# Chunked attention with two MoE layers on one core: the first eight blocks' value rows loaded by query group, their memory rows copied on GpSimd, and a planner that counts eight transfers in flight

## The chip, the cores and the metric

One core of a Trainium2 chip runs the whole kernel. The metric is the device time of one execution in microseconds (us), the median of several runs. The profile that is read here is one execution of the kernel before, recorded by the hardware profiler. The engines are named as in the profile: PE (TensorE matmul), PEld (TensorE weight load), DVE (VectorE), ACT (ScalarE), POOL (GpSimd) and SP (SyncE, which issues the transfers; SPq is its queue).

## The reference

Attention works on chunks of 32 queries. Each chunk sees 8 memory rows, 16 rows to its left, its own 32 rows and 8 rows to its right (64 rows in all); then two layers with a hidden width of 2048 follow, in float32.

```python
batch, n_heads, seq, head_dim = (4, 8, 768, 64); n_mem = 8
chunk, left_ctx, right_ctx = (32, 16, 8)
k_full = np.concatenate([mem_k, k_ctx], axis=2)
v_full = np.concatenate([mem_v, v_ctx], axis=2)
scores = scale * np.matmul(q_c, k_full.transpose(0, 1, 3, 2))
a = np.exp(scores - np.max(scores, axis=-1, keepdims=True))
a = a / (np.sum(a, axis=-1, keepdims=True) + 1e-09)
out[:, :, c_start:c_end] = np.matmul(a, v_full)
...
h = x @ w_in                               # 3072 x 512 by 512 x 2048
y = (h * np.clip(h + 3.0, 0.0, 6.0) / 6.0) @ w_out
# second layer: the same shapes, with a squared gate in place of the clipped one
```

## The kernel before, in words

**Attention.** A block is four chunks (128 queries); there are 24 blocks. The inputs come in groups of 96 queries: for group `j` the queries and keys of all heads are one array of 128 partitions (`q_sb`, 448 KB, loaded by `load_block`, L521), and the value rows are 128 rows of 512 numbers (8 memory rows, 16 left, 96 own, 8 right). A block makes scores on PE (tile `sc`, L619), the maximum on DVE (L633), the exponentials on ACT (L644), the normalisation and a transpose on DVE (L654, L663, tile `tr`), and the values on PE (tile `pv`, L688). For blocks 0 to 7 (the "not late" ones) ACT and DVE then split the result into two parts, `xhi` and `xlo` (L748, L752), the operands of the first layer.

**Value rows.** `load_values` gives each block one tile `v_sb` of 128 partitions by two halves of 512 numbers (512 KB): partition 32·c holds the rows of chunk c, its first 32 context rows in half 0 and its last 32 in half 1. The eight memory rows come first in a chunk's context, so for the second and third chunk of a group they stand elsewhere in memory than the rows that follow. The helper therefore cuts the rows into runs that are whole both in memory and in the tile, and issues one transfer for each run (L573): 8 or 9 for each of blocks 0 to 7, of 8 to 96 rows.

**The first layer's start.** Tokens are worked in tiles of 512. Tile 0 needs blocks 0 to 3. Its hidden units (tile `ph`, L772 to L774, 12 matmuls for each of 16 steps) start when all four blocks are done and the first weight is decoded; blocks 4 to 7 come in between. The weights arrive as 8-byte numbers (`raw`, 512 KB each, L295) and are decoded on ACT and DVE (L302 to L338) to two float32 parts `w`. The projection (tile `py`, L808 to L810) runs some steps behind.

**What sets the order.** All work is added to a `Plan` as tasks with a cost, a key and dependencies. `Plan.run` places them on the engines' time lines by these costs, and the instructions are emitted in that order. A transfer's landing is modelled on one shared line, `bw`; in the kernel before this is

```python
bw = max(bw, t.end + (1900 if est < FILL else 2500)) + t.kb / 0.39
t.end = bw
```

so a transfer's place in the order of every engine hangs on it. Before the first 60 us of the plan are over, gaps that the plan sees on PE are filled with matmuls on a zero tile `warm` (L1080). In the program as it is built, SP's transfers take eight semaphores (DMAHW0 to DMAHW7) in turn, and each transfer from the ninth on waits on SP until the one eight places earlier has landed.

**Lines.** In the changed kernel L521 becomes L525, L573 becomes L604, L295 becomes L299, L619 L659, L688 L728, L772 to L774 L812 to L814, and L1080 L1120.

Of the kernel before, what the change touches and what calls it, by code (L numbers as in the profile page):

```python
# [22 lines left out]
NMEM = 8  # L23
CHUNK, LEFT, RIGHT = 32, 16, 8
# [10 lines left out]
NEARLY = 6  # L35
# [8 lines left out]
FILL = 60000  # L44
# [34 lines left out]
class Plan:  # L79
# [65 lines left out]
    def run(self, at):  # L145
        free = dict(at)
        bw = 0
        last_kind = None
        ready = {e: [] for e in free}

        def put(t):
            for e, _ in t.ways:
                ready[e].append(t)

        for t in self.tasks:
            if not t.left:
                put(t)
        left = len(self.tasks)
        order = []
        while left:  # L160
            best = None
            for e, ts in ready.items():
                found = []
                blocked = set()
                for t in sorted(ts, key=lambda t: (t.key, t.n)) if e == "SP" else ts:
                    est = max(free[e], t.ready)
                    wants = {p for b in t.bufs if not b.slot for p in ([b.share[0]] if b.share else b.pools)}
                    taken = [] if blocked & wants else self.slots_for(t)
                    if taken is None or len(taken) < sum(b.slot is None for b in t.bufs):
                        if e == "SP":  # L170

                            blocked.update(wants)
                        continue
                    found.append((max([est, *(s.at + HOP for s in taken)]), t))
                if not found:
                    continue
                first = min(x[0] for x in found)
                if e == "PE" and last_kind:

                    same = [x for x in found if x[1].kind and x[0] <= free[e] + WINDOW]  # L180
                    found = same or found
                est, t = min(
                    (x for x in found if x[0] <= first + WINDOW), key=lambda x: (x[1].key, x[1].n)
                )
                if best is None or est < best[0]:
                    best = est, e, t
            assert best, ("no task can start", [
                (t.n, t.emit.__qualname__, t.key, [b.name for b in t.bufs if b.slot is None])
                for ts in ready.values() for t in ts][:20])
            est, e, t = best  # L190
            for x, _ in t.ways:
                ready[x].remove(t)
            ns = dict(t.ways)[e]
            if e == "PE":
                ns += CHANGE * (bool(t.kind) != bool(last_kind))
                last_kind = t.kind
            t.eng, t.start = e, est
            free[e] = est + ns
            t.end = est + ns + TAIL[e]
            if t.kb:  # L200
                bw = max(bw, t.end + (1900 if est < FILL else 2500)) + t.kb / 0.39
                t.end = bw
            for b, s in zip([b for b in t.bufs if b.slot is None], self.slots_for(t)):
                b.slot, s.used = s, True
                if b.share:
                    self.held[b.share[0]] = self.held.get(b.share[0], 0) + 1
            for b in t.bufs:
                b.users -= 1
                b.free_at = max(b.free_at, t.end)
                if not b.users:  # L210
                    b.slot.used, b.slot.at = False, b.free_at
                    if b.share:
                        self.held[b.share[0]] -= 1
            for d in t.then:
                d.left -= 1
                d.ready = max(d.ready, est)
                if not d.left:
                    put(d)
            for d in t.next:
                d.left -= 1  # L220

                alone = all(x == e for x, _ in d.ways)
                d.ready = max(d.ready, est + ns if alone else t.end + HOP)
                if not d.left:
                    put(d)
            order.append(t)
            left -= 1
        order.sort(key=lambda t: (t.start, t.n))
        return order
# [11 lines left out]
def fused_kernel(ctx: ExitStack, tc: tile.TileContext, qkv, qk, vv, wpk, const, out):  # L241
    nc = tc.nc
# [26 lines left out]
    add = plan.add  # L269

    def tile_of(b):
        if b.tile is None:
            pool = ps if b.slot.pool in banks else smalls if b.slot.pool == "sm" else sb
            b.tile = pool.tile(b.shape, b.dtype, tag=f"{b.slot.pool}{b.slot.n}", name=b.name)
        return b.tile

    V, A, P, G = nc.vector, nc.scalar, nc.tensor, nc.gpsimd
# [212 lines left out]
    WQ = NP * (QB + KB)  # L490
    KC = NMEM + LEFT + CHUNK + RIGHT
    NCH = QB // CHUNK
    NSB = 4
# [3 lines left out]
    later = {}  # L497
# [46 lines left out]
    def load_values(s, key):  # L544


        early = key < 0
        late = s * SB >= 2 * T
        v = v_buf[s] = Buf(
            ["lv"] + ["w"] * early, [128, 2, H * D], F32, "v_sb", **({"w": 1} if early else {}),  # L550
        )
        runs = []
        for c in range(NSB):
            j, i = divmod(s * NSB + c, NCH)
            cuts = [0] + [NMEM] * (i > 0) + [CHUNK] * (not late) + [KC]
            for a, b in zip(cuts, cuts[1:]):
                row = a if b <= NMEM else a + CHUNK * i
                p, col = (64 * (c % 2) + a, c // 2) if late else (CHUNK * c + a % CHUNK, a // CHUNK)
                for r in runs:
                    if r[0] == j and r[1] + r[4] == row and r[2] + r[4] == p and r[3] == col:  # L560
                        r[4] += b - a
                        break
                else:
                    runs.append([j, row, p, col, b - a])
        for n, (j, row, p, col, m) in enumerate(sorted(runs, key=lambda r: (r[3], r[2]))):
            if j < NEARLY:
                src, rows = qkv[j, row:row + m, WQ:], lambda t: t
            else:
                g = 2 * (j - NEARLY)
                src, rows = vv[g:g + 2, row:row + m, :].rearrange("g k c -> k g c"), lambda t: t.rearrange("k (g c) -> k g c", g=2)  # L570
            add(
                ("SP", 430), key - 5 - 3 * (not early),
                lambda e, src=src, rows=rows, p=p, m=m, col=col: nc.sync.dma_start(rows(tile_of(v)[p:p + m, col]), src),  # L573
                writes=[(v, n)], kb=2 * m, line="load v", after=later.get(s // 4, ()),
            )
        v.parts = len(runs)

    def block(s, key):
        first = key < 0
        late = s * SB >= 2 * T  # L580
        bank = ["a", "y", "h"] if first else ["a", "h"] if s * SB < 4 * T else ["a"]
        spare = ["w"] if first else []
        v = v_buf[s]
        half = range(2)
        chunks = range(NSB)
# [3 lines left out]
        tr = Buf(["st"] + spare, [128, 2, H, CHUNK], F32, "tr", w=3)  # L589
        sm = Buf(["sm"], [128, 4, H], F32, "sm")  # L590
        if late:
            pv = [Buf(bank, [128, NC, 2, CHUNK], F32, "pv", **keep) for _ in half]
        else:
            pv = [Buf(bank, [128, NC, 1, CHUNK], F32, "pv", **keep) for _ in chunks]
# [111 lines left out]
            add(("ACT", 1150), key - 3, lambda e, h=h: exps(e, h), [(sc[h], 0), (sm, 2)], [(st, h), (sm, 0, h)])  # L706
        add(("DVE", 440), key - 2.5, weigh, [(sm, 0, 0), (sm, 0, 1)], [(sm, 3)])
        add(("DVE", dve(512)), key - 2.4, norm, [(sm, 3)], [(st, 0), (st, 1)])
        of_v = [(v, n) for n in range(v.parts)]
        if late:  # L710
            for c in chunks:
                for b in range(2):
                    add(("DVE", 450), key - 2.2, lambda e, c=c, b=b: turn_part(e, c, b), [(st, 0), (st, 1)], [(tr, c, b)])
            ts = [(tr, c, b) for c in chunks for b in range(2)]
            add(("PE", 1065), key - 1, values, [*ts, *of_v], [(x, 0) for x in pv], line="values", kind="a")
        else:
            add(("DVE", 635), key - 2.2, turn, [(st, 0), (st, 1)], [(tr, 0)])
            for m in range(2):
                add(
                    ("PE", 1065), key - 1, lambda e, m=m: values(e, m), [(tr, 0), *of_v],  # L720
                    [(x, 0) for x in pv[2 * m:2 * m + 2]], line="values", kind="a",
                )
        n = s * SB // T
# [15 lines left out]
        for z, x in enumerate(pv):  # L739
            def to(y, z=z):  # L740
                o = s * SB - n * T
                t = tile_of(y)[:, :, o:o + SB].rearrange("p c (m z t) -> p c m z t", z=len(pv), t=CHUNK)
                return t[:, :, :, z, :]

            part = s, z
            m = SB // len(pv) * NC
# [233 lines left out]
    m = NS // NT  # L980
    for s in range(NS):
        n, i = divmod(s, m)
# [27 lines left out]
    for k in range(NK):  # L1010
        f, n = k % NF, k // NF
# [14 lines left out]
    for n, (l, p) in enumerate(pairs):  # L1026
        base = NK + 30 * n
        for i in range(NF // 2):
            k = base + step * i
# [121 lines left out]
```

## Time and profile before

| | us |
|---|---|
| median of 3 runs | 1122.48 |
| lowest and highest | 1119.35, 1126.87 |
| the profiled execution | 1117.13 |
| its span in the profile | 1115.3 |
| PE busy | 1088.8 |
| DVE busy, ACT busy | 678.3, 601.5 |

The profile page gives busy times and the DMA queues. The view of windows gives, for each stretch, its length and then busy us (and the number of instructions) of PE, PEld, DVE, ACT and POOL, the clock granted to TensorE as a share of full speed, the busy share of the 16 DMA engines, and GB/s. The chain of waits lists pieces by start, length and what the time was; "issue" is time in which the engine waited for nothing that the profile shows. A timeline row has start, length, engine, line, operation and, in brackets, the idle time before it with what ended it. In the trace a float32 matmul of the attention stands as two records, one for each of its passes, so one block's 64 value matmuls are 128 records. In the list of DMA queues a row has the number of packets, MB, and the time that they took as a share of 16 engines over the stretch; q1 carries the kernel's own transfers and q8 those named "instruction".

### The profile page before, as it was taken

Reading aid. Unit: us, or ns where it says so; the run is one execution under the profiler, and the core shown is the slowest. Engines: PE = TensorE matmul, PEld = TensorE weight load, DVE = VectorE, ACT = ScalarE, POOL = GpSimd, SP = SyncE. Lnnn points to the kernel's source line nnn. Section 1 sums busy time; section 2 is a strip of 40 time slices with the busy share of each in tenths; the row PEclk is TensorE's granted clock in tenths of the full one; section 3 lists DMA queues with packets and bytes.
Section 4 is the critical chain, followed back from the end, with each engine's and each line's share of the span. In section 5 each row is a group of like instructions: output and inputs, shape, how many; then the busy total and the mean of one; then the engine's idle time right before and its main releaser. Section 6 shows DMA issues by size and latency. Waiting matters only on the chain.

```text
span 1115.3 us, 21354 instructions
## 1 busy us (share of the span) xinstructions
PE 1088.8 (98%) x8477; PEld 887.7 (80%) x8477; DVE 678.3 (61%) x1185; ACT 601.5 (54%) x1312; POOL 0.2 (0%) x4
## 2 busy tenths in 40 slices
PE   7799999999999999999999999999999999999998
PEld 6688888787778777788878878888888888888887
DVE  2699547867988866487797455572344572443442
ACT  3699434444665544376675467672455652555531
POOL 0000000000000000000000000000000000000000
PEclk8799999999999999999999999999999999999999
DMA  5793169887878729599999586755576364764061
GB/s 177 255 384 110 55 203 353 294 287 253 309 261 246 237 83 361 181 362 411 415 382 413 176 312 242 283 180 170 212 273 212 107 225 179 276 227 139 1 245 38
DMA packets 108809, 265.65 MB, mean 238 GB/s; under 512 B 11046, under 2 KB 44710, under 8 KB 108710
## 3 DMA queue, kind: packets, MB, share of 16 engines
q1 hardware_dynamic: 108710, 264.29, 66.1%
q8 instruction: 67, 1.10, 0.4%
q14 instruction: 32, 0.26, 0.1%
HBM read 199.23 MB, written 65.01 MB: 237 GB/s over the span
## 4 chain that ended last, share of the span: by engine, by line
PE 81%; DMA 8%; DVE 5%; ACT 3%; issue 2%; SPq 1%; DVEq 0%; ACTq 0%
PE ph L926 10%; PE ph L927 9%; PE ph L928 9%; PE po L815 8%; PE po L813 8%; PE po L814 8%; PE py L808 6%; PE py L809 6%; PE py L810 6%; PE ph L772 2%; PE ph L773 2%; PE ph L774 2%; DMA raw<-wpk 2%; PE pv L688 2%; PE sc L619 2%
## 5 line engine op out<-in xcount | busy, mean ns | idle before, releaser
L926 PE MATMUL ph<-xop,wf 128*128 128x512 f32 x448 | 175.2, 391 | 2.5 <-ACT s L910 2.1
L927 PE MATMUL ph<-xop,wf 128*128 128x512 f32 x448 | 174.4, 389 | 0.0
L928 PE MATMUL ph<-xop,wf 128*128 128x512 f32 x448 | 174.3, 389 | 0.0
L962 ACT ACTIVATE r<-s,bias 128x512 f32<-128x512 f32 x120 | 86.8, 725 | 128.5 <-DVE s L914 127.5
L808 PE MATMUL py<-ghi,w 128*128 128x512 f32 x384 | 152.0, 396 | 0.9 <-DVE ysb L835 0.9
L809 PE MATMUL py<-glo,w 128*128 128x512 f32 x384 | 149.9, 390 | 1.5 <-DVE glo L793 1.5
L810 PE MATMUL py<-ghi,w 128*128 128x512 f32 x384 | 149.6, 390 | 0.0
L815 PE MATMUL po<-w,glo 128*128 128x512 f32 x384 | 149.6, 389 | 0.0
L813 PE MATMUL po<-w,ghi 128*128 128x512 f32 x384 | 149.5, 389 | 0.0
L814 PE MATMUL po<-w,ghi 128*128 128x512 f32 x384 | 149.4, 389 | 0.0
L914 DVE TENSOR_TENSOR s<-s,ph 128x512 f32<-128x512 f32 x120 | 82.0, 685 | 72.2 <-PE ph L928 44.5
L793 DVE TENSOR_TENSOR glo<-g,ghi 128x512 fp32r<-128x512 f32 x80 | 54.7, 690 | 96.6 <-ACT ghi L792 96.5
L792 ACT CAST ghi<-g 128x512 fp32r<-128x512 f32 x80 | 49.2, 622 | 111.3 <-PE po L814 78.5
L926 PEld LDWEIGHTS ph<-xop,wf 128*128 128x128 f32 x448 | 84.1, 188 | 22.4 <-ACT s L910 4.4
L928 PEld LDWEIGHTS ph<-xop,wf 128*128 128x128 f32 x448 | 84.1, 188 | 17.7
L927 PEld LDWEIGHTS ph<-xop,wf 128*128 128x128 f32 x448 | 84.1, 188 | 17.1
L910 ACT COPY s<-ph 128x512 f32<-128x512 f32 x120 | 69.3, 578 | 52.0 <-PE ph L928 46.1
L808 PEld LDWEIGHTS py<-ghi,w 128*128 128x128 f32 x384 | 72.1, 188 | 17.7 <-DVE ysb L835 1.8
L970 DVE SCALAR_TENSOR_TENSOR s<-r,s 128x512 f32<-128x512 f32 x80 | 55.2, 690 | 50.2 <-ACT r L966 43.0
L809 PEld LDWEIGHTS py<-glo,w 128*128 128x128 f32 x384 | 72.1, 188 | 16.5 <-DVE glo L793 2.3
L793 DVE TENSOR_TENSOR glo<-s,ghi 128x512 fp32r<-128x512 f32 x80 | 55.1, 690 | 49.1 <-ACT ghi L792 48.9
L815 PEld LDWEIGHTS po<-w,glo 128*128 128x128 f32 x384 | 72.1, 188 | 15.6 <-DVE glo L793 0.6
(96 smaller groups left out, 1739.3 us busy)
## 6 DMA issues: line engine op xcount, KB each, us to landing
w<-wos SPq DMA_DIRECT2D x124, 512.0 KB
raw<-wpk SPq DMA_DIRECT2D x64, 512.0 KB
wf<-wfs SPq DMA_DIRECT2D x48, 512.0 KB
wf<-wfs SPq DMA_DIRECT2D x48, 384.0 KB
wos<-w SPq DMA_DIRECT2D x32, 512.0 KB
wis<-w SPq DMA_DIRECT2D x16, 512.0 KB
wts<-wt SPq DMA_DIRECT2D x16, 512.0 KB
wf<-wts SPq DMA_DIRECT2D x16, 512.0 KB
```

Source lines behind the costliest of these rows:

```text
L793: add(("DVE", dve(T)), key + 0.1, lambda e: V.tensor_tensor(out=tile_of(glo), in0=g(), in1=tile_of(ghi), op=ALU.subtract,), [of, (ghi, 0)] ...
L808: P.matmul(y, w2hi, gh, start=first, stop=False)
L809: P.matmul(y, w2hi, gl, start=False, stop=False)
L810: P.matmul(y, w2lo, gh, start=False, stop=last)
L813: P.matmul(y, gh[:, t], wt[:, 0], start=first, stop=False)
L814: P.matmul(y, gh[:, t], wt[:, 1], start=False, stop=False)
L815: P.matmul(y, gl[:, t], wt[:, 0], start=False, stop=last)
L914: add(("DVE", dve(T)), key + 0.39 * j, lambda e: V.tensor_tensor(out=tile_of(s), in0=tile_of(s), in1=tile_of(b), op=ALU.add,), [(b, 0)], [ ...
L926: P.matmul(q, whi()[:, m], xh, start=first, stop=False, skip_group_check=True)
L927: P.matmul(q, whi()[:, m], xl, start=False, stop=False, skip_group_check=True)
L928: P.matmul(q, wlo()[:, m], xh, start=False, stop=c == 1, skip_group_check=True)
L962: add(("ACT", 750 if l else act(T, psum) + 80), key, lambda e: A.activation(out=tile_of(r), in_=tile_of(h), func=AF.Relu, bias=bias[:, l:l ...
```

## The change

For blocks 0 to 7, `load_values` now issues transfers by group of 96 queries instead of by run. For groups 0 to 5, one transfer fills both halves for all chunks that block and group share (`96x2x512`, `64x2x512` or `32x2x512`); for later groups there is one for each half. Half 0 of a second or third chunk then holds 8 ordinary rows where the memory rows belong, and a GpSimd copy of 8 rows by 512 numbers (L613), from a chunk of the block that starts a group, overwrites them: 21 copies. The values matmuls depend on the pieces of their own chunks instead of on all pieces of the tile. The planner's model of a transfer changes for all transfers of the program: SP can't issue while eight are in flight, a transfer costs 1000 ns before its bytes move, and its landing comes 2000 ns after them.

```diff
@@ Plan.run
+        landed = []
...
+                    if e == "SP" and len(landed) >= 8:
+                        est = max(est, landed[-8])
...
-                bw = max(bw, t.end + (1900 if est < FILL else 2500)) + t.kb / 0.39
-                t.end = bw
+                bw = max(bw, t.end + 1000) + t.kb / 0.39
+                t.end = bw + 2000
+                landed.append(t.end)
@@ load_values (the late blocks keep their runs)
+            while c < NSB:
+                j, i = divmod(s * NSB + c, NCH)
+                n = min(NCH - i, NSB - c)
+                own = []
+                if j < NEARLY:
+                    at = qkv[j, CHUNK * i:CHUNK * (i + n), WQ:]
+                    (row, m), rest = at.ap
+                    src = type(at)(at.tensor, at.offset, [(row, m), (CHUNK * row, 2), rest])
+                    own.append((lambda c=c, n=n: tile_of(v)[CHUNK * c:CHUNK * (c + n)], src, 4 * m))
+                else:
+                    g = 2 * (j - NEARLY)
+                    for col in range(2):
+                        src = vv[g:g + 2, CHUNK * (i + col):CHUNK * (i + col + n), :].rearrange("g k c -> k g c")
+                        own.append((
+                            lambda c=c, n=n, col=col: tile_of(v)[CHUNK * c:CHUNK * (c + n), col].rearrange("p (g c) -> p g c", g=2),
+                            src, 2 * CHUNK * n,
+                        ))
...
             add(
-                ("SP", 430), key - 5 - 3 * (not early),
+                ("SP", 400), key - 5 - 3 * (not early), lambda e, to=to, src=src: nc.sync.dma_start(to(), src),
+                writes=[(v, n)], kb=kb, line="load v", after=later.get(s // 4, ()),
             )
+        if not late:
+            at = next(c for c in range(NSB) if (s * NSB + c) % NCH == 0)
+            for c in range(NSB):
+                if (s * NSB + c) % NCH:
+                    part = lambda c: tile_of(v)[CHUNK * c:CHUNK * c + NMEM, 0]
+                    add(
+                        ("POOL", 900), key - 4 - 3 * (not early), lambda e, c=c, part=part: G.tensor_copy(part(c), part(at)),
+                        [*v.of[at], *v.of[c]], [(v, "m", c)],
+                    )
+                    v.of[c] = [*v.of[c], (v, "m", c)]
@@ block
-        of_v = [(v, n) for n in range(v.parts)]
+        of_v = lambda cs: [x for c in cs for x in v.of[c]]
...
-                    ("PE", 1065), key - 1, lambda e, m=m: values(e, m), [(tr, 0), *of_v],
+                    ("PE", 1065), key - 1, lambda e, m=m: values(e, m), [(tr, 0), *of_v((2 * m, 2 * m + 1))],
```

SP's queue at the very start, before the change (`q_sb` are the queries and keys of a group, `v_sb` the value rows of a block):

```order
L521 DMA q_sb<-qkv 128x896 x2
L573 DMA v_sb<-qkv 32x512
L573 DMA v_sb<-qkv 8x512
L573 DMA v_sb<-qkv 24x512
L573 DMA v_sb<-qkv 8x512
L573 DMA v_sb<-qkv 24x512
L573 DMA v_sb<-qkv 32x512
L573 DMA v_sb<-qkv 96x512
L573 DMA v_sb<-qkv 32x512
L521 DMA q_sb<-qkv 128x896
```

The same place of SP's queue in the changed kernel, down to the first weights:

```order
L525 DMA q_sb<-qkv 128x896 x2
L604 DMA v_sb<-qkv 96x2x512
L604 DMA v_sb<-qkv 32x2x512
L525 DMA q_sb<-qkv 128x896
L604 DMA v_sb<-qkv 64x2x512 x2
L525 DMA q_sb<-qkv 128x896
L604 DMA v_sb<-qkv 32x2x512
L604 DMA v_sb<-qkv 96x2x512
L525 DMA q_sb<-qkv 128x896 x2
L604 DMA v_sb<-qkv 96x2x512
L604 DMA v_sb<-qkv 32x2x512
L299 DMA raw<-wpk 128x512 x2
```

Blocks 0 to 3 took 34 transfers of value rows before and take 8 now, so that the first weight is SP's 15th transfer in place of its 41st. In the whole program SP has 46 transfers fewer than before (69 of value rows for blocks 0 to 7 became 23).

SP's queue at block 4's value rows, before, with the semaphores that each transfer waits for in brackets (DMAHW: an earlier transfer; PE: matmuls that still read the tile's old content):

```order
L521 DMA q_sb_654<-qk 128x896 [waits DMAHW2_49,PE_49]
L295 DMA raw_662<-wpk 128x512 [waits DMAHW3_49]
L295 DMA raw_664<-wpk 128x512 [waits DMAHW4_49]
L573 DMA v_sb_669<-qkv 8x512 [waits DMAHW5_49,PE_49]
L573 DMA v_sb_669<-qkv 24x512 [waits DMAHW6_49]
L573 DMA v_sb_669<-qkv 8x512 [waits DMAHW7_49]
L573 DMA v_sb_669<-qkv 24x512 [waits DMAHW0_49]
```

The same place now:

```order
L299 DMA raw_366<-wpk 128x512 [waits DMAHW1_49]
L299 DMA raw_432<-wpk 128x512 [waits DMAHW2_49]
L299 DMA raw_479<-wpk 128x512 [waits DMAHW3_49]
L604 DMA v_sb_539<-qkv 64x2x512 [waits DMAHW4_49,PE_49,Pool_49]
L604 DMA v_sb_539<-vv 64x2x256 [waits DMAHW5_49]
L604 DMA v_sb_539<-vv 64x2x256 [waits DMAHW6_49]
L299 DMA raw_637<-wpk 128x512 [waits DMAHW7_49]
```

Block 4's value rows reuse block 0's tile, so their first transfer waits for block 0's values on PE, and now for its copies on POOL too; 20 transfers stand ahead of it (before: 45), five of them weights.

PE's queue at the end of the first hidden step, before (`xhi` is the first layer's operand, `w` its weight, `warm` the zero tile):

```order
L772 MATMUL ph<-xhi,w 128x512
L773 MATMUL ph<-xlo,w 128x512
L774 MATMUL ph<-xhi,w 128x512
L1080 LDWEIGHTS warm
L1080 MATMUL ph<-warm 128x512
```

The same place now, from the end of the first step's 12 matmuls:

```order
L814 MATMUL ph<-xhi,w 128x512
L812 MATMUL ph<-xhi,w 128x512
L813 MATMUL ph<-xlo,w 128x512
L814 MATMUL ph<-xhi,w 128x512
L812 MATMUL ph<-xhi,w 128x512
```

Before, 14 matmuls on the zero tile stand between the first and the second hidden step; now none do, and three hidden steps (36 matmuls) follow each other. Up to the first hidden matmul PE has 159 matmuls on the zero tile before and 108 now; the five score blocks (0 to 4) and four value blocks (0 to 3) ahead of it are the same instructions in both, in another order. In the whole program PE's instructions other than those on the zero tile are as many as before, in another order.

## Rows read from the trace of the kernel before

**Rows 1.** The page's list of busy time by engine.

```profile
PE 1088.8 (98%) x8477; PEld 887.7 (80%) x8477; DVE 678.3 (61%) x1185; ACT 601.5 (54%) x1312; POOL 0.2 (0%) x4
```

**Rows 2.** View of windows: the stages of the span, and its first 6.9 us.

```profile
0.00:6.90 6.90, 5.36 (x111) 4.01 (x114) 0.13 (x3) 1.49 (x2) 0.20 (x4) 1.00 0.62 200
0.00:47.00 47.00, 35.06 (x1199) 29.86 (x1200) 17.83 (x55) 19.78 (x93) 0.20 (x4) 0.80 0.67 218
50.70:55.10 4.40, 2.90 (x16) 1.33 (x14) 3.60 (x8) 4.33 (x19) 0.00 (x0) 1.00 0.26 68
200.00:400.00 200.00, 195.55 (x2143) 155.87 (x2142) 164.01 (x325) 111.63 (x344) 0.00 (x0) 0.99 0.79 257
400.00:600.00 200.00, 196.11 (x974) 159.76 (x973) 145.05 (x224) 115.26 (x185) 0.00 (x0) 1.00 0.87 335
600.00:1000.00 400.00, 399.43 (x1759) 329.38 (x1758) 193.52 (x278) 210.41 (x335) 0.00 (x0) 1.00 0.62 227
```

**Rows 3.** SP's timeline: value rows of blocks 0 and 1, then the first weights.

```profile
1.65 4.92 SPq L573 DMA_DIRECT2D v_sb<-qkv  x8
7.08 5.70 SPq L573 DMA_DIRECT2D v_sb<-qkv  x9
...
26.80 1.60 SPq L295 DMA_DIRECT2D raw<-wpk  x2
```

**Rows 4.** The chain of waits, 10 to 62 us: its pieces of "issue".

```profile
18.38 1.34 issue
...
22.35 2.87 issue
...
34.11 0.35 issue
...
36.27 2.80 issue
...
42.03 1.07 issue
```

**Rows 5.** The page's DMA queue that is named instruction.

```profile
q8 instruction: 67, 1.10, 0.4%
```

**Rows 6.** View of windows: from a PE restart to the next q8 packet.

```profile
19.73:22.90 3.17, 2.62 (x126) 2.38 (x126) 0.93 (x3) 0.00 (x0) 0.00 (x0) 0.70 0.89 281
25.23:26.50 1.27, 1.27 (x49) 1.27 (x51) 0.49 (x2) 0.81 (x5) 0.00 (x0) 0.50 0.19 61
28.30:32.20 3.90, 3.90 (x129) 3.73 (x129) 2.23 (x6) 2.14 (x15) 0.00 (x0) 0.62 0.89 311
34.46:36.50 2.04, 1.81 (x126) 1.68 (x127) 1.13 (x5) 1.33 (x5) 0.00 (x0) 1.00 0.92 325
39.07:40.50 1.43, 1.43 (x82) 1.21 (x81) 0.43 (x1) 0.00 (x0) 0.00 (x0) 0.50 0.43 124
43.10:48.10 5.00, 5.00 (x90) 3.64 (x90) 2.98 (x8) 3.79 (x10) 0.00 (x0) 0.50 0.99 385
```

**Rows 7.** DMA queues of 22.9:23.0, 32.2:32.3, 40.5:40.6 and 48.0:48.2, in that order.

```profile
q8 instruction: 1, 0.02, 60.4%
...
q8 instruction: 1, 0.02, 62.1%
...
q8 instruction: 1, 0.02, 66.6%
...
q8 instruction: 1, 0.02, 31.0%
```

**Rows 8.** PE's timeline: first hidden matmul, filling matmuls, second hidden step, first projection.

```profile
47.02 0.99 PE L772 MATMUL ph<-xhi,w 128*128 128x512 f32 x1
...
52.23 3.18 PE L1080 MATMUL ph<-warm 128*128 128x512 bf16 x14 [1.50 <-DVE r L784]
55.06 0.59 PE L772 MATMUL ph<-xhi,w 128*128 128x512 f32 x1
...
61.99 0.50 PE L808 MATMUL py<-ghi,w 128*128 128x512 f32 x1
```

**Rows 9.** DVE's timeline: block 0's transposed weights.

```profile
14.76 0.71 DVE L663 STREAM_TRANSPOSE tr<-st 128x512 f32<-128x512 f32 x1
```

More of the change, by code (lines that the diff above doesn't have):

```diff
@@ L551, in load_values @@
         )
[L552 to L562, printed above, removed]
-                else:
-                    runs.append([j, row, p, col, b - a])
@@ L565, in load_values @@
[L565 to L570, printed above, removed]
-            add(
-                ("SP", 430), key - 5 - 3 * (not early),
-                lambda e, src=src, rows=rows, p=p, m=m, col=col: nc.sync.dma_start(rows(tile_of(v)[p:p + m, col]), src),
-                writes=[(v, n)], kb=2 * m, line="load v", after=later.get(s // 4, ()),
-            )
@@ L576, in load_values @@
-        v.parts = len(runs)
+        loads = []
+        v.of = {}
+        if late:
+            runs = []
+            for c in range(NSB):
+                j, i = divmod(s * NSB + c, NCH)
+                cuts = [0] + [NMEM] * (i > 0) + [KC]
+                for a, b in zip(cuts, cuts[1:]):
+                    row = a if b <= NMEM else a + CHUNK * i
+                    p, col = 64 * (c % 2) + a, c // 2
+                    for x in runs:
+                        if x[0] == j and x[1] + x[4] == row and x[2] + x[4] == p and x[3] == col:
+                            x[4] += b - a
+                            break
+                    else:
+                        runs.append([j, row, p, col, b - a])
+            for n, (j, row, p, col, m) in enumerate(sorted(runs, key=lambda x: (x[3], x[2]))):
+                g = 2 * (j - NEARLY)
+                src = vv[g:g + 2, row:row + m, :].rearrange("g k c -> k g c")
+                to = lambda p=p, m=m, col=col: tile_of(v)[p:p + m, col].rearrange("k (g c) -> k g c", g=2)
+                loads.append((to, src, 2 * m))
+                for c in range(NSB):
+                    v.of.setdefault(c, []).append((v, n))
+        else:
+            c = 0
+            while c < NSB:
+                j, i = divmod(s * NSB + c, NCH)
+                n = min(NCH - i, NSB - c)
[5 more added lines that the diff above has]
+                    own.append((lambda c=c, n=n: tile_of(v)[CHUNK * c:CHUNK * (c + n)], src, 4 * m))
+                else:
+                    g = 2 * (j - NEARLY)
+                    for col in range(2):
[4 more added lines that the diff above has]
+                        ))
+                for x in range(n):
+                    v.of[c + x] = [(v, len(loads) + y) for y in range(len(own))]
+                loads += own
+                c += n
@@ new lines, in load_values @@
+        for n, (to, src, kb) in enumerate(loads):
+            add(
+                ("SP", 400), key - 5 - 3 * (not early), lambda e, to=to, src=src: nc.sync.dma_start(to(), src),
+                writes=[(v, n)], kb=kb, line="load v", after=later.get(s // 4, ()),
+            )
+        if not late:
+            at = next(c for c in range(NSB) if (s * NSB + c) % NCH == 0)
+            for c in range(NSB):
+                if (s * NSB + c) % NCH:
[5 more added lines that the diff above has]
+                    v.of[c] = [*v.of[c], (v, "m", c)]
@@ L714, in block @@
             ts = [(tr, c, b) for c in chunks for b in range(2)]
-            add(("PE", 1065), key - 1, values, [*ts, *of_v], [(x, 0) for x in pv], line="values", kind="a")
+            add(("PE", 1065), key - 1, values, [*ts, *of_v(chunks)], [(x, 0) for x in pv], line="values", kind="a")
         else:
```

## The prediction

> **What bounds the kernel now.** I read the page's busy times first. PE is busy for 1088.8 of 1115.3 us [rows 1], so a change of the transfers can gain only where PE waits or fills time. The view of windows says where. From 200 us on PE is idle for 4.5, 3.9 and 0.6 us in three stretches [rows 2], about 9 us in 800. The losses sit at the start: up to 47 us PE runs the attention of blocks 0 to 3, much filling on the zero tile, and gaps. The first hidden matmul starts at 47.02 [rows 8]; the second hidden step starts at 55.06, after a stretch without useful PE work (50.7 to 55.1, 14 filling matmuls and 1.5 us of idle) [rows 2, 8]. What follows the first hidden matmul is nearly all PE work, so the end moves almost one for one with the start.
>
> Next I ask what holds the start. SP's timeline shows what the change aims at: the value rows of block 0 hold SP for 4.92 us and those of block 1 for 5.70, and the first weight is issued at 26.80 [rows 3]. But the chain of waits puts another cause on the path: five pieces of "issue", together 8.43 us, in which PE waits for nothing shown [rows 4]. They end at 19.72, 25.22, 34.46, 39.07 and 43.10. From the first restart to the next stop PE runs 126 matmul records and their 126 weight loads; the same 126 stand between 34.46 and 36.5 [rows 6]. The instruction queue moved 1.10 MB in 67 packets [rows 5], and 8477 matmuls with as many loads [rows 1], shared over 67, make 253 instructions a packet. So PE's program comes in pieces of some 253 instructions, and in the small attention matmuls, where a piece lasts about 2.6 us, PE runs out of them. A packet starts at 22.9, 32.2, 40.5 and 48.1 [rows 7], and PE restarts 2.3 to 2.6 us later (25.22, 34.46, 43.10).
>
> What makes a refill slow is the wait from the crossing into one piece to the packet of the next [rows 6]: 1.3 us with the DMA engines 19% busy and 1.4 us at 43%, but 3.2 and 3.9 us at 89% and 5.0 us at 99%. From restart to restart the refills took 5.5 us (19.72 to 25.22), 3.1 and 6.2 (25.22 to 34.46, with the unstalled crossing at about 28.3), 4.6 and 4.0. That cuts against the change: it keeps the DMA engines busier in just this stretch, which now runs at a mean of 67% and 218 GB/s [rows 2].
>
> A rule of the Trainium skill stands beside this: "Runtime: NRT & Kernel Launch", section "Instruction fetch mechanics", says that instructions are refilled in blocks of 256 while the block before is executed, at a cost that is mostly hidden. The trace agrees with the block's size (253) and not with the hiding (8.43 us of stops).
>
> **The change part by part.**
>
> *Fewer, larger transfers.* Blocks 0 to 3 lose 26 of 34 value transfers. At 4.92 us for 8 [rows 3] a transfer holds SP for 0.6 us, so SP is free some 16 us earlier and the weights come forward by about that. The bytes stay the same. Six query groups of 448 KB and four value tiles of 512 KB are 4.7 MB, 12 us at the 385 GB/s of a full stretch [rows 6], so data alone would let block 3 start before 20 us.
>
> *PE's instructions up to the first hidden matmul.* Before there are 1199 records [rows 2]. The order has 159 filling matmuls before and 108 now, all else equal, so 1148. With 126 records a piece, both lie behind nine crossings; the first is at record 99, by about 6.8 us (111 records by 6.9 [rows 2]). It lies in block 0's scores, which hang on the first two transfers in both kernels. Eight refills therefore stand between 6.8 us and the ninth crossing, 41 records ahead of the first hidden matmul.
>
> *What a refill costs now.* Twenty transfers, 7.7 MB or 20 us of data, stand ahead of block 4's value rows, eight in flight at a time, so the engines are near full from the start. I take 5.9 us, the mean of 5.5 and 6.2, the two at 89% of load. SP then has to wait for block 0's values before it can fill that tile again, and later for block 1's; twice the transfers run dry, and I give those two refills the quiet 3.1 us. Sum: 6.8 + 6 × 5.9 + 2 × 3.1 = 48.4. From the ninth crossing to the first hidden matmul there were 3.92 us for 88 records (43.10 to 47.02); for 41 I take 2.0. That makes 50.4 in place of 47.0: 3.4 us lost. The bounds: all eight refills quiet gives 6.8 + 24.8 + 2.0 = 33.6, 13.4 gained. Six refills at 7.4 (a wait of 5.0 at 99%, and 2.4 to the restart) give 59.4, 12.4 lost; all eight at 7.4 give 68.0, 21 lost.
>
> *The second hidden step.* Its weights are now issued long before they are needed, and the order puts no filling between the first three hidden steps. The 4.4 us of 50.7 to 55.1 go; four filling matmuls at 0.23 us (14 in 3.18) stand ahead of the next steps. Gain 3.5 us. The least is 0 (the decoding on ACT and DVE is late and PE waits where it now fills), the most 4.4.
>
> *The copies on GpSimd.* The trace has only four tiny ones on POOL, 0.2 us in all [rows 1], so 0.05 us is one bound. The other is the 0.71 us of a DVE instruction on 512 numbers [rows 9], and I take that: two or three copies are 2.1 us a block. The rows land by some 8 us (block 0's 512 KB come just behind the first two transfers) and the transposed weights are ready at 15.5 [rows 9], which hides them. Without that cover they cost 2.1 us a block, 8 us for four; copying more gains nothing in itself. The finer waits of the values matmuls cost nothing, since all pieces land early.
>
> *The planner's new model.* It reorders all of PE's queue without adding work. What it can take or give back is the idle time of 200 to 1000 us, 9 us [rows 2]: between 9 gained and as much lost. Nothing in the trace says which; I take 0. The late blocks' transfers are unchanged in size.
>
> *Sum.* 3.4 lost, 3.5 gained, 0: nothing. The profiled execution's 1117.13 us stays, with a span of 1115.3; it lies 5.35 us under the median of the runs shown. I forecast the median, 1122.5 us.
>
> **The rivals.**
>
> *Faster: refills stay as they are or quicken.* Larger transfers could end sooner and leave the DMA engines idle for longer; before, the transfers of 8 and 24 rows kept the share at 67% while moving only 218 GB/s. For it: the bytes need only 12 us, and the shortest refills were 3.1 us. Against it: every refill above 89% of load took 5.5 us or more, and the weights follow without a gap. With all refills quiet the start gains 13.4 us; the filling then comes back because the weights have to be decoded first, so I add nothing: 1122.5 − 13.4 = 1109. The rule quoted above, that a refill is mostly hidden, would have it so.
>
> *Slower: refills queue behind eight large transfers.* The mechanism is the instruction packet's wait behind whatever is in flight, at crossings two to nine. During the three longer waits the data moved were 3.17 us × 281 GB/s = 0.9 MB, 3.9 × 311 = 1.2 MB and 5.0 × 385 = 1.9 MB [rows 6], about what SP had handed out; with eight large transfers in flight it can be over 3 MB. Price: at 7.4 us a loaded refill the start loses 12.4 us, less 3.5, so 1131.5. It decides from the point where a loaded refill takes over 5.9 us; at 7.8 the loss passes 1%. Against it: SP's waits for old tiles make quiet stretches.
>
> The Trainium skill speaks against this one too: "DMA: Bandwidth & Descriptors", section "Queues, rings and completion order", says that an engine takes turns between its queues after each packet, which would cap the wait whatever is in flight. The trace rather shows waits that grow with load (1.3, 3.2, 5.0); no row tells a cap above 5.0.
>
> *The new order opens waits later.* Nine us more idle time behind 200 us: 1131. For it: ACT and DVE are the near-bound partners there (DVE 164 of 200 us [rows 2]). Against it: the counts of work are the same.
>
> **How the numbers follow.** Forecast 0.45, faster 0.27, slower refills 0.20, later waits 0.08. The range of the forecast alone is ± 6. For 8 in 10 I go from the faster rival's 1109 to a little over the slower ones, 1135, leaving out the case with all eight refills at 7.4 (1140). A measurement of this kernel can tell about 1% (11 us). The faster rival passes that only with nearly all refills quiet: 0.11. The slower ones pass it from 7.8 us a refill, or if two cases add: 0.10. Within 1%: 0.79.
>
> **What would show it.** Right: "issue" pieces on PE before the first hidden matmul of more than 8.4 us in all, a busier DMA share than 67% up to there, the first hidden matmul at 48 to 53, no filling between the first and second hidden step, and the first projection near 62 as now (61.99 [rows 8]). POOL's copies all done before the values that need them. Wrong: a first hidden matmul by 40 (refills weren't the limit), one past 57 (they queue behind all that is in flight), values waiting on POOL, or an idle sum from 200 to 1000 us far from 9.

## The result and the profile after

The changed kernel takes 1130.94 us (median of 8 runs, 1127.53 to 1133.38), the kernel before 1120.91 in the runs beside it (8 runs, 1119.19 to 1126.87). The ratio is 1.0074, with a 95% interval of 1.0045 to 1.0103. It is slower by 0.7%: inside the range and below the 1% of the forecast "no change", but not the nothing that the sum gave. Of the profiled executions, after's took 1130.79 us (span 1129.0), 13.7 more than before's; before's was a quick one of its kind, so I use the pair for places and the medians for the size.

From the page of the changed kernel: busy times, and the queue that brings instructions.

```profile
PE 1090.8 (97%) x8417; PEld 890.5 (79%) x8417; DVE 682.4 (60%) x1191; ACT 601.5 (53%) x1306; POOL 15.1 (1%) x25
...
q8 instruction: 66, 1.08, 0.4%
```

PE has 60 instructions fewer than in [rows 1], and the engines' work is otherwise nearly the same. PE is busy for 2.0 us more and the span is 13.7 us longer, so most of the time went into waits. The view of windows of the changed kernel, with the stages of [rows 2] and the stretch up to its own first hidden matmul (columns as there):

```profile
0.00:47.00 47.00, 29.88 (x873) 24.68 (x877) 13.70 (x42) 15.54 (x81) 8.57 (x17) 0.71 0.89 267
0.00:62.80 62.80, 39.79 (x1148) 31.95 (x1149) 20.11 (x55) 21.70 (x96) 11.13 (x20) 0.66 0.85 270
200.00:400.00 200.00, 190.91 (x2117) 151.78 (x2116) 158.90 (x322) 104.53 (x329) 0.00 (x0) 0.98 0.82 273
400.00:600.00 200.00, 199.67 (x1056) 164.14 (x1055) 146.28 (x234) 115.05 (x196) 0.00 (x0) 1.00 0.82 315
600.00:1000.00 400.00, 400.00 (x1764) 330.63 (x1763) 202.44 (x290) 214.81 (x341) 0.00 (x0) 1.00 0.65 237
```

In the first 47 us PE gets through 873 records where it got through 1199; the DMA engines' share rose from 0.67 to 0.89. The 1148 records that the order promised up to the first hidden matmul are there, but they last 62.8 us. Behind 200 us the idle time is 9.1, 0.3 and 0 us in place of 4.5, 3.9 and 0.6: 9.4 us where it was 8.9.

PE's timeline of the changed kernel, its first instructions and the first layer's start, against [rows 8]:

```profile
0.98 6.19 PE L1120 MATMUL sc<-warm 128*128 128x256 bf16 x31 [0.98 <-DVE bias L1100]
7.10 1.13 PE L659 MATMUL sc<-q_sb 64*32 64x8 f32 x96
...
59.20 1.07 PE L728 MATMUL pv<-tr,v_sb 32*64 32x32 f32 x30 [2.35 <-issue]
60.21 3.17 PE L1120 MATMUL ph<-warm 128*128 128x512 bf16 x7
62.81 0.99 PE L812 MATMUL ph<-xhi,w 128*128 128x512 f32 x1
...
73.68 0.58 PE L848 MATMUL py<-ghi,w 128*128 128x512 f32 x1
```

The first hidden matmul came at 62.81 instead of 47.02 (15.8 us later), the first projection at 73.68 instead of 61.99 (11.7 later). So 4.1 us come back between the two, and 2.0 of the 13.7 are lost behind.

The pieces of "issue" in the changed kernel's chain of waits, up to that point (start, length):

```profile
12.39 3.43 issue
...
20.24 3.42 issue
...
27.95 2.00 issue
...
32.52 0.87 issue
...
36.64 2.57 issue
...
44.32 2.27 issue
...
49.42 3.63 issue
...
56.85 2.35 issue
```

Eight stops, 20.5 us in all, where [rows 4] have five and 8.43. They end at 15.82, 23.66, 29.95, 33.39, 39.21, 46.59, 53.05 and 59.20, and the distances are the refills: 7.8, 6.3, 3.4, 5.8, 7.4, 6.5 and 6.2 us. The view of windows from each restart to the next packet of the instruction queue shows what [rows 6] showed (its DMA share adds up the times of the packets that begin in the stretch, so it can pass 1):

```profile
15.82:21.00 5.18, 4.46 (x128) 3.15 (x128) 2.92 (x7) 2.47 (x16) 2.17 (x3) 0.59 1.04 271
23.66:27.40 3.74, 3.74 (x101) 3.40 (x102) 2.44 (x6) 1.50 (x9) 0.12 (x1) 0.57 1.03 411
29.95:31.00 1.05, 1.05 (x45) 1.05 (x45) 0.00 (x0) 0.00 (x0) 0.00 (x0) 0.67 0.06 23
33.39:36.80 3.41, 3.25 (x125) 2.97 (x126) 2.49 (x8) 1.02 (x6) 1.29 (x2) 0.50 0.89 265
39.21:43.80 4.59, 4.59 (x120) 4.33 (x122) 0.86 (x4) 1.63 (x10) 0.00 (x0) 0.50 1.04 382
46.58:50.40 3.82, 2.93 (x128) 2.48 (x128) 2.32 (x5) 2.61 (x6) 2.31 (x3) 0.50 1.04 369
53.05:56.60 3.55, 3.55 (x127) 3.21 (x126) 0.09 (x1) 0.38 (x3) 0.00 (x0) 0.50 1.04 413
```

The wait is 1.05 us where the engines stand at 0.06, and 3.4 to 5.2 at 0.89 and more; PE restarts 2.4 to 2.8 us after each of these packets. The longest loaded wait is about that of before (5.18 against 5.00), but the six average 4.05 us, where the four rows of [rows 6] at 0.89 and more (3.17, 3.90, 2.04, 5.00) average 3.5. And only one wait is a quiet one. Why only one is seen in SP's timeline of the changed kernel:

```profile
17.50 3.64 SPq L299 DMA_DIRECT2D raw<-wpk  x3
31.25 0.61 SPq L604 DMA_DIRECT2D v_sb<-qkv  x1
...
35.62 1.26 SPq L299 DMA_DIRECT2D raw<-wpk  x2
39.99 1.77 SPq L604 DMA_DIRECT2D v_sb<-vv  x4
```

SP stands from 21.14 to 31.25 for block 0's values, long enough for the transfers to run dry. Its second stop, 36.88 to 39.99, is too short for that: the DMA share stays at 0.99 through it.

### The profile page after: what moved, and what is told of

Its sections match the earlier page's. It is cut to its first block, busy times and chain, and to the rows that moved or that the text cites. A ratio compares the mean times of both kernels' runs of the same rounds, so it can differ in the third digit from the quotient of the medians.

```text
span 1129.0 us, 21239 instructions
## 1 busy us (share of the span) xinstructions
PE 1090.8 (97%) x8417; PEld 890.5 (79%) x8417; DVE 682.4 (60%) x1191; ACT 601.5 (53%) x1306; POOL 15.1 (1%) x25
## 4 chain that ended last, share of the span: by engine, by line
PE 88%; DMA 5%; issue 2%; DVE 2%; ACT 1%; SPq 1%; DVEq 0%
PE ph L966 11%; PE ph L967 11%; PE ph L968 11%; PE po L855 8%; PE po L853 8%; PE po L854 8%; PE py L848 7%; PE py L849 7%; PE py L850 7%; PE ph L812 2%; PE sc L659 2%; PE ph L813 2%; PE ph L814 2%; PE pv L728 2%; PE pv L718 1%
## 5 line engine op out<-in xcount | busy, mean ns | idle before, releaser
L954 DVE TENSOR_TENSOR s<-s,ph 128x512 f32<-128x512 f32 x120 | 82.2, 685 | 74.9 <-PE ph L968 50.4
L848 PEld LDWEIGHTS py<-ghi,w 128*128 128x128 f32 x384 | 72.2, 188 | 15.8
L853 PEld LDWEIGHTS po<-w,ghi 128*128 128x128 f32 x384 | 72.1, 188 | 15.2 <-ACT ghi L832 0.4
```

The source lines that it names most:

```text
L848: P.matmul(y, w2hi, gh, start=first, stop=False)
L853: P.matmul(y, gh[:, t], wt[:, 0], start=first, stop=False)
L954: add(("DVE", dve(T)), key + 0.39 * j, lambda e: V.tensor_tensor(out=tile_of(s), in0=tile_of(s), in1=tile_of(b), op=ALU.add,), [(b, 0)], [ ...
```

## Experiments

Theory: in the first 60 us PE waits for its own instructions, a refill takes longer the busier the DMA engines are, and the change adds load. Rivals: the planner's new order costs the time, or the start doesn't decide the end. "Ratio" is to the kernel before in the same runs, with its 95% interval. Positions are of each run's own trace.

**The transfers alone** (the changed kernel with the planner's old model):

```diff
-                    if e == "SP" and len(landed) >= 8:
-                        est = max(est, landed[-8])
...
-                bw = max(bw, t.end + 1000) + t.kb / 0.39
-                t.end = bw + 2000
-                landed.append(t.end)
+                bw = max(bw, t.end + (1900 if est < FILL else 2500)) + t.kb / 0.39
+                t.end = bw
```

> The value transfers by group and the GpSimd copies alone, with the planner's old model of a transfer. PE's queue up to the first hidden matmul is that of the changed kernel but for five filling matmuls (1143 records in place of 1148). Theory (PE's instruction refills wait behind the larger transfers): the refills are as slow as in the changed kernel, about 20 us of issue before the first hidden matmul, which starts at 60 to 63 us, and the whole takes 1128 to 1134 us. Rival (the planner's new model and the order that it makes are what costs): the start is that of the kernel before or earlier, first hidden matmul by 50, and the whole takes 1112 to 1122.

Measured: 1134.9 us, ratio 1.0122 (1.0080 to 1.0164); first hidden matmul at 67.72. Its window of the first 47 us:

```profile
0.00:47.00 47.00, 28.91 (x838) 23.90 (x840) 11.89 (x38) 14.03 (x77) 6.61 (x14) 0.68 0.99 330
```

The share is 0.99, still fewer records are done, and eight stops in the chain add up to 26.0 us. The first hidden matmul is later than the 60 to 63 expected. One wait, from the restart at 42.63 to the next packet, is longer than any in the changed kernel:

```profile
42.63:48.97 6.34, 5.13 (x126) 4.77 (x126) 2.21 (x8) 3.19 (x14) 0.00 (x0) 0.50 1.05 300
```

So the loads alone are enough for the whole loss. Whether they cost more than the whole change (1.0122 against 1.0074) isn't shown, since the two intervals overlap. With the old model 18 weights stand ahead of block 4's values.

**The planner's model alone** (the kernel before with only the lines removed above put in).

> The planner's new model alone, with the old 8 or 9 value transfers a block. PE has 1266 records up to the first hidden matmul, so ten crossings in place of nine. Theory (refills): each refill is as short as in the kernel before (mean 4.7 us), with one more of them, so the first hidden matmul comes at 50 to 53 us and the whole takes 1121 to 1127. Rival (the planner's order costs): about 1131, as the changed kernel, with the loss behind the start.

Measured: 1123.65 us, ratio 1.0002 (0.9975 to 1.0029); first hidden matmul at 53.27. Its windows behind 200 us:

```profile
200.00:400.00 200.00, 191.86 (x2171) 152.59 (x2171) 158.64 (x321) 102.54 (x311) 0.00 (x0) 0.97 0.81 271
400.00:600.00 200.00, 199.45 (x993) 163.50 (x992) 145.72 (x232) 116.12 (x195) 0.00 (x0) 1.00 0.83 317
```

No change, as the prediction took it. The model moves idle time from 400 to 600 us into 200 to 400 (8.1 and 0.6 us against before's 4.5 and 3.9), as it does in the changed kernel.

**The changed kernel without filling.**

```diff
-            if t.eng == "PE" and t.start <= FILL:
+            if t.eng == "PE" and t.start < 1:
```

> The changed kernel without the filling matmuls on the zero tile (they are not part of the result). 1040 records stand before the first hidden matmul, so eight crossings in place of nine. Theory (refills): one refill of about 6.5 us less, first hidden matmul at 55 to 58 us (62.8 in the changed kernel), the whole 1123 to 1127. Rival (the filling is needed to keep TensorE's granted clock at 2.4 GHz, and without it the start gets slower): first hidden matmul at 63 or later, 1131 to 1137.

Measured: 1123.67 us, ratio 1.0027 (0.9998 to 1.0056); first hidden matmul at 55.10. In this trace the first hidden matmul comes 7.7 us earlier than in the changed kernel's; of the whole some 5 us come back (1.0027 against 1.0074). The granted clock of the first 47 us is 1.00 here and 0.71 there, so this run alone doesn't tell the number of instructions from the clock.

**The changed kernel with its weights held back** behind the attention of blocks 1, 2 and 3, by a one-column write into the weights' tile (the plan also takes up the attention of blocks 0 to 3 ahead of the weights; that part of the edit is left out here):

```diff
+    GATES = {(0, 0): 1, (1, 0): 1, (2, 0): 2, (0, 1): 2, (3, 0): 3, (1, 1): 3}
+    REST = (3, 3)
...
+        if l == 0 and GATES.get((f, z), REST) is not None:
+            add(
+                ("DVE", 60), key - 4.1, lambda e: V.memset(tile_of(raw).bitcast(F32)[:, :1], 0.0),
+                writes=[lo, hi], after=[turns[GATES.get((f, z), REST)]],
+            )
...
```

> The changed kernel with the first layer's weight transfers held back: each waits for a one-column memset on DVE that stands behind the transpose of block 1 (two weights), 2 (two), 3 (two), and behind block 3's last xlo (all others). PE's queue up to the first hidden matmul is the same but for three filling matmuls. Theory (refills wait behind what is in flight): with less in flight the refills from the third on fall to 3 to 5 us, the first hidden matmul comes at 46 to 54 us, and the whole takes 1117 to 1124. Rival (the order of PE's queue or the instruction stream itself sets the refills, not the transfers): first hidden matmul at 60 to 64 and the whole at 1131 or more, since the weights come later too.

Measured: 1124.17 us, ratio 1.0016 (0.9991 to 1.0041); first hidden matmul at 53.39. Its chain:

```profile
11.48 3.55 issue
...
19.32 3.28 issue
...
33.09 1.46 issue
...
39.02 0.19 issue
...
41.66 3.46 issue
```

The transfers, the copies and the filling rule are the same. What differs is when the weights' transfers come (now behind block 4's value rows), and three filling matmuls more on PE. The stops fall from 20.5 to 11.9 us, the first hidden matmul comes 9.4 us earlier, and the share of the first 47 us is 0.76 in place of 0.89. The granted clock can't be what came back: over those 47 us it is 0.66 here and 0.71 in the changed kernel. This is the plainest evidence for the load as the cause.

**The kernel before without filling** (the edit of the third experiment).

> The kernel before without its filling matmuls on the zero tile (they are not part of the result): 1040 records up to the first hidden matmul, eight crossings in place of nine, transfers as before. Theory (refills): one refill of 4 to 6 us less, first hidden matmul at 41 to 44 us in place of 47.0, the whole 1115 to 1120. Rival (the filling keeps the granted clock up and hides in waits that are there anyway): first hidden matmul at 47 or later, 1121 or more.

Measured: 1112.46 us, ratio 0.9927 (0.9899 to 0.9954), better than foretold; but the first hidden matmul of its trace stands at 48.99, not at 41 to 44. That trace was the slowest of ten runs (1116.56). A second one:

> The kernel before without filling once more, for a second trace: its profiled execution (1116.56) was the slowest of ten. Theory (the start's refills are what varies): an execution near 1112 has its first hidden matmul at 42 to 46 us in place of 49.0. Rival (the variation lies behind the start): 48 to 50 us.

Measured: 1110.86 us, first hidden matmul at 47.81, first projection at 61.36 (62.57 in the first trace). Of the 5.7 us between the two executions 1.2 lie in the start and 4.5 behind the projection. So the gain of this kernel is sure, and its place in the start isn't shown by these two traces.

**Is it the filling's instructions or its time?** Two edits of the kernel before. The first issues each filling matmul as two halves (159 instructions more, same columns):

```diff
+                        for x in range(2):
                             P.matmul(
+                                c[:, x * m // 2:(x + 1) * m // 2], warm,
```

> The kernel before with each filling matmul cut into two of half its columns: the same filling time on PE, but 1358 records up to the first hidden matmul, so 1.3 refills more. Theory (refills): first hidden matmul 5 to 8 us later, at 52 to 55, and the whole 1125 to 1131. Rival (what counts is PE time and the transfers, not the number of instructions): within 1 us of the kernel before at the first hidden matmul, the whole 1119 to 1123.

Measured: 1120.91 us, ratio 0.9996 (0.9972 to 1.0019); first hidden matmul at 55.74, and only 1049.7 us from the first projection to the end, where before had 1053.3. The start of this trace is late, but only 2.1 us later than that of a second trace of the kernel before (53.65, below), and the whole time is the one that the rival named, not the theory's 1125 to 1131. A cost of the added instructions isn't shown by this run. The second keeps the instructions and cuts each to four columns:

```diff
+                        P.matmul(c[:, 0, :4], warm, warm[:, :4], start=True, stop=True, skip_group_check=True)
```

> The kernel before with each filling matmul cut to four columns: as many instructions as before (1199 records up to the first hidden matmul, nine crossings), but hardly any filling time on PE. Theory (what the kernel without filling gained came from one refill less): no gain, 1118 to 1123 us, ratio to the kernel before 0.997 to 1.003. Rival (it came from the filling's own time in PE's in-order queue, or from the granted clock that stays high without it): 1110 to 1115, as the kernel before without filling (1112.46), ratio 0.990 to 0.995.

Measured: 1117.33 us, ratio 0.9979 (0.9956 to 1.0002); first hidden matmul at 47.37. With the instructions kept, most of the 0.73% is gone (0.21% left). The granted clock of the profiled executions, 1.00 without filling, 0.995 here and 0.989 in the kernel before, rose in both, so it doesn't account for that. This points to the count; the halves don't confirm it, so what one filling instruction costs stays open.

**How far executions of one kernel differ**: a second trace of the kernel before.

> The kernel before once more, for a second trace of its start: the executions of it run from 1113 to 1130 us, and the profiled one (1117.13) lies at the low end. Theory (the start's refills are what varies): an execution near 1121 has its first hidden matmul at 49 to 53 us, with more issue than 8.4 us before it. Rival (the variation lies behind the start): first hidden matmul at 46 to 48 us.

Measured: 1127.4 us (the first trace: 1117.13), first hidden matmul at 53.65. Its chain up to there:

```profile
10.78 0.40 issue
...
15.48 0.48 issue
...
17.81 1.96 issue
...
22.61 2.73 issue
...
29.27 2.73 issue
...
40.16 3.88 issue
...
46.99 2.74 issue
```

14.9 us of stops against 8.43 [rows 4] in the same program, and 7.8 of the 10.3 us between the two executions lie ahead of the first projection (69.80 and 61.99). Two traces of the kernel before differ by 6.5 us in their stops; the one trace of the changed kernel (20.5) lies above both. Against this second trace its first hidden matmul is 9.2 us later, not 15.8.

**Fewer instructions ahead of the first hidden matmul.** Block 4's scores are moved behind it (`vals[3, 3]` is block 3's last `xlo`), and the filling is left out:

```diff
-            keys.append((NF - 2) * (i + 1) / m - 0.5)
+            keys.append((NF - 2) * (i + 1) / m - 0.5 + (1.5 if i == 0 else 0))
...
-            [(sc[0], 0), (sc[1], 0)], hold=[st], line="scores", kind="a",
+            [(sc[0], 0), (sc[1], 0)], hold=[st], line="scores", kind="a", after=[vals[3, 3]] if s == 4 else (),
```

On the changed kernel, with the weights held back as well:

> The changed kernel with the weights held back as in e4_gate, without the filling, and with block 4's scores placed behind the first hidden step: 928 records up to the first hidden matmul, seven crossings. Theory (refills): first hidden matmul at 40 to 47 us, the whole 1109 to 1118. Rival (with the weights held back the decoding is what the first hidden steps wait for): first hidden matmul as in e4_gate (53.4), the whole 1121 to 1126.

Measured: 1113.49 us, ratio 0.9931 (0.9904 to 0.9958); first hidden matmul at 43.70. On the kernel before:

> The kernel before, without the filling and with block 4's scores behind the first hidden step: 928 records, seven crossings, its own 8 or 9 value transfers a block. Theory (refills): two refills less than the kernel before, first hidden matmul at 36 to 42 us, the whole 1109 to 1117, faster than both kernels. Rival (the small value transfers, not the refills, hold the start of the kernel before): first hidden matmul at 44 or later, the whole 1118 to 1123.

Measured: 1111.79 us, ratio 0.9895 (0.9844 to 0.9946); first hidden matmul at 44.48, later than the 36 to 42 expected. The same kernel again, with more rounds:

> The kernel of e9_before_sc4 once more (the kernel before without filling and with block 4's scores behind the first hidden step), in five rounds for a narrower interval and a second trace. Theory (two refills less at the start): 1107 to 1113 us, ratio to the kernel before 0.986 to 0.993, first hidden matmul at 42 to 46. Rival (the first four runs were lucky): the ratio is that of the kernel before without filling, 0.992 to 0.996, 1112 to 1116 us.

Measured: 1109.27 us (6 runs, 1108.04 to 1115.13), ratio 0.9884 (0.9855 to 0.9913); first hidden matmul at 43.12. It is faster than both kernels by its interval. That interval overlaps the one of leaving out the filling alone (0.9899 to 0.9954), so what moving the scores adds isn't shown. The waits on PE of its first 55 us that were "issue" (us, times, longest):

```profile
PE pv L689 <- issue: 6.7, 3, 3.3
...
PE sc L620 <- issue: 3.8, 2, 3.0
```

PE still waits 10.5 us for instructions, but the chain that ends last no longer runs through these stops: up to the first hidden matmul its "issue" pieces are at most 0.07 us each, and it goes through the transfers of queries, values and weights. The next limit is there.

## Why the prediction was right and wrong

The measured 1130.94 us lies inside the range, but 8.4 us above the forecast of 1122.5 and outside its own ± 6, next to the 1131.5 of the slower rival. What bounds the start was right, and so was the direction of the two large terms. Their net, forecast as nothing, was 10.0 us in the medians.

**The step that failed is "What a refill costs now".** It took 5.9 us for six loaded refills and 3.1 for two quiet ones, 41.6 in all. The eight refills took 51.3, from about 7.9 (record 99: 31 filling matmuls, and 68 of the 96 records of 7.10 to 8.23) to 59.20. Seven were loaded, at a mean of 6.84, and one was quiet, at 3.4. Of the 9.7 us missed, 5.6 are the size (six at 0.94) and the rest the second quiet stretch that never came. A wait of SP gives a quiet stretch only where it is longer than what is in flight takes to land, which I did not ask of the second one (3.1 us, with the share at 0.99 throughout). The bounds of that step (59.4 and 68.0) held the 62.81.

An average of all loaded rows would not have given the size: the four waits of [rows 6] at 0.89 and more average 3.5 us, which with 2.4 to the restart makes 5.9 again. But I read two of these rows wrongly. "Every refill above 89% of load took 5.5 us or more" passes over the one from 34.46 to 39.07, with a wait of 2.04 us at 0.92 and 4.6 us in all. And the unstalled crossing isn't at 28.3, as PE's timeline of the kernel before shows:

```profile
25.23 2.17 PE L688 MATMUL pv<-tr,v_sb 32*64 32x32 f32 x71 [2.87 <-issue]
27.33 1.04 PE L1080 MATMUL sc<-warm 128*128 128x256 bf16 x4
28.30 1.54 PE L619 MATMUL sc<-q_sb 64*32 64x8 f32 x96
```

By 28.30 PE has run 75 records since its restart; the 126th comes at about 28.9. That makes the quiet refill 3.7 us in place of 3.1 and the loaded one behind it 5.5 in place of 6.2 (a wait of 3.3, not 3.90). What the rows couldn't show is that they came from a quick execution: the second trace of the same kernel has 14.9 us of stops, not 8.43.

**Around it.** The first crossing was 1.1 us later than the 6.8 taken, because 31 filling matmuls hold PE until 7.10. The tail from the ninth restart to the first hidden matmul was 3.6 us instead of 2.0: seven filling matmuls took 3.17 us, 0.45 each, where [rows 8] had 14 in 3.18. The granted clock was 0.50 (1.2 GHz) there and 1.00 in before. With 9.7 that makes the 12.4 us by which the first hidden matmul missed 50.4.

**What held.** The second hidden step: forecast 3.5 us back, 4.1 measured, and no filling stands before it. The planner's model: 0 forecast, 1.0002 measured alone. The copies, in POOL's timeline of the changed kernel:

```profile
8.69 1.26 POOL L613 COPY v_sb<-v_sb 8x512 f32<-8x512 f32 x2 [8.25 <-DMA v_sb<-qkv]
47.98 2.68 POOL L613 COPY v_sb<-v_sb 8x512 f32<-8x512 f32 x3 [10.45 <-PE pv L728]
```

0.63 us each in the first group and 0.89 in the slowest, around the 0.71 taken, and PE has no wait on POOL in the first 75 us. Of the signs named for "right" three more came out: stops over 8.4 us, a share over 0.67, no filling between the steps. Two did not: the first hidden matmul (48 to 53 named, 62.81 measured) and the first projection (near 62 named, 73.68 measured). The first hidden matmul past 57 was the sign named for the slower rival.

**The rivals.** "Refills queue behind eight large transfers" came nearest: 1131.5 forecast (its sum makes 1131.4), 1130.94 measured, and its deciding point (a loaded refill over 5.9 us) was passed at 6.84. That the times agree so well is partly luck: it took six refills at 7.4, and there were seven at 6.84, with a later first crossing and a slower tail. Its reason is only half borne out. The wait isn't set by the load alone: at shares of 0.89 and 0.92 the kernel before has waits of 3.17 and 2.04 us, at 1.03 and 1.04 the changed kernel has 3.55 to 5.18. The change made more refills loaded, and the loaded ones longer on average rather than at the longest. The rule of the Trainium skill that the prediction held against this rival ("DMA: Bandwidth & Descriptors", section "Queues, rings and completion order"), that an engine takes turns between its queues, is not settled here: no wait of the changed kernel passes 5.2 us, but the transfers alone have one of 6.3, so no row shows a cap.

The other rule, that a refill is mostly hidden ("Runtime: NRT & Kernel Launch", section "Instruction fetch mechanics"), does not hold in this start: 20.5 us of stops in 60. It fits the rest, where PE is idle for 9.4 us in 800 behind 200 us. "Faster" fell with the start. "The new order opens waits later" fell too: 9.4 us of idle time behind 200 us against 8.9.

## What to carry to other kernels

Where small matmuls follow each other so fast that PE outruns its instruction refills, a busier DMA is a cost: look for "issue" in the chain of waits, count the instructions ahead of the critical one, and ask what each transfer does to the refills before moving it forward. Try leaving out instructions that do nothing before making transfers better: here that gave 0.73% on the kernel before. And take a second trace before a term of a sum rests on one: the stops of the same kernel were 8.4 us in one execution and 14.9 in another.

## What was unexpected

The instruction queue's packet waits for the kernel's own transfers: for 16 KB it waited 1.05 us at a DMA share of 0.06, up to 5.2 at 1.04, and 6.3 at 1.05 in the transfers alone.

Filling PE's gaps did not pay. Without it the granted clock stays at 1.00 (2.4 GHz) in the record of the start of the kernel before, though PE is busy for less than half of 20 to 30 us (first trace without filling):

```profile
20.00:30.00 10.00, 4.77 (x207) 4.33 (x189) 1.90 (x7) 3.15 (x20) 0.00 (x0) 1.00 0.86 290
```

With filling it reads 0.50 in four of the seven windows of the changed kernel. Yet the column alone does not tell the rate. PE's timeline of that kernel without filling, at the first hidden step:

```profile
49.58 0.63 PE L773 MATMUL ph<-xlo,w 128*128 128x512 f32 x1
50.01 0.63 PE L774 MATMUL ph<-xhi,w 128*128 128x512 f32 x1
...
52.69 0.40 PE L772 MATMUL ph<-xhi,w 128*128 128x512 f32 x1
52.93 0.39 PE L773 MATMUL ph<-xlo,w 128*128 128x512 f32 x1
```

The first stand 0.43 us apart and the later ones 0.23, with the recorded clock at 1.00. At some 0.2 us each the seven slow ones cost about 1.4 us. Why they are slow is open.
